# Attention and snake MLP on one core: moving one chunk's TensorE transposes from the first stage into the first product

## The chip, the cores and the metric

The kernel runs on one core of a Trainium2 chip. The metric is the time of one execution on the device, in microseconds (us), and lower is better. Four runs of the kernel before are shown: 437.31, 437.31, 438.04 and 438.66, with a median of 437.67.

The engines are named as the profile names them: PE is TensorE's matmul side and PEld its weight loads, DVE is VectorE, ACT is ScalarE, POOL is GpSimd, and SP issues most of the DMAs. Each engine works through its own instructions in the order in which the program has them.

## The reference

The inputs are q, k and v with 8 batches, 12 heads, 448 tokens and a head size of 64, two gain vectors g_q and g_k, and an MLP of 768 by 2048 and back.

```
q_n = q / sqrt(mean(q*q) + 1e-6) * g_q         # k_n likewise with g_k
attn = softmax(q_n @ k_n.T / 8) @ v            # per batch and head
x = attn as 3584 tokens x 768
h = x @ w_in                                   # 2048 wide
g = h + sin(alpha * h)**2 / alpha
out = g @ w_out
```

Matmuls take bf16 inputs and accumulate in f32.

## The kernel before

The 12 heads of a batch form 6 pairs of heads, and two pairs form a chunk, so a batch has 3 chunks (`NC` = 3) and the whole input has 24. Chunks are numbered through all batches: chunks 0 to 2 belong to the first batch, chunk 3 is the first one of the second batch, and in the code of the first stage c0 to c4 are the norms of chunks 0 to 4. In the change's title "fourth chunk" is chunk 3.

For each chunk the norm runs in steps: squares of q and k, sums of squares (`reduce`, L227, on DVE), the reciprocal root (`rsqrt`, L236 and L237, on ACT), folding both gains into q (L224, POOL), scaling (L246), and a transpose, so that the head dimension lies on the partitions (`qkT`). The first four chunks are transposed on PE (`pe_transpose`, L260 to L277): 28 transposes of 64x64 blocks into one PSUM bank pair `tp`, and two DVE copies from there to `qkT`. All later chunks go through a DMA transpose.

`scores` (L286) makes one of 7 key tiles of a chunk: four matmuls into a bank pair `sc`, and one exponential on ACT (L297) that writes `expT`. A batch has 21 of these score tiles. `attend` (L302) makes the values of one pair: per key tile four matmuls (the values and the row sums) that accumulate in a bank pair `av`, then `rec` (logarithm and exponential on ACT, L320 and L321) and two DVE multiplies that write `xT` (L326). In the program, `S_` is a score tile (a number in it adds that many warming matmuls on zeros), `A_()` is the values of one pair and `A_(2)` the values of the last two pairs interleaved.

`first_product` (L346), called h(b), makes h for a batch: 16 column tiles of 128, two to a bank pair `hps`, 6 matmuls each. The first two bank pairs are filled together, k-tile by k-tile, because the last `xT` come late. Each h tile goes through `snake`: a sine on ACT (L332), a square on POOL or ACT, and a DVE instruction that writes `g_sb` (L340) one h tile later. Tasks given in `beside` are emitted after the numbered pair of h tiles. `second_product` (L379) makes the output from `g_sb` and `w_out`; its matmuls (`ops`, L400) are the fillers of the next batch's stage, and each unit ends with a DVE copy `osb` (L406) and output DMAs.

PSUM is cut into four bank pairs. `bank_pair` (L97) hands out the one that is due first by times that the code itself adds up (`clock`, `passes`, `give_back`); an instruction that needs a bank still in use waits for it on the chip.

The first stage, batch 0's scores and values, is written out by hand (L484 to L532), and so is the order on PE, ACT and DVE there. From batch 1 on, the order within a stage is the string `PLAN` (L535), 83 items long; norm tasks of later chunks hang on 24 slots spread evenly over it. In the stage of batch b, n3 and n4 are the first two chunks of batch b + 1, whose norms are made beside it; their steps 3 and 4 are the two sums of squares (for q and for k).

Of the kernel before, what the change touches and what calls it, by code (L numbers as in the profile page):

```python
# [32 lines left out]
def kernel(  # L33
# [33 lines left out]
    NJ = S // REST  # L67
# [29 lines left out]
    def bank_pair(name, dtype=F32):  # L97
        slot = min(free_at, key=free_at.get)
        clock["pe"] = max(clock["pe"], free_at.pop(slot))
        ps = psum.tile([P, 2, 2048 // mybir.dt.size(dtype)], dtype, tag=f"ps{slot}", name=name)  # L100
        slot_of[id(ps)] = slot
        return ps

    def passes(pe=0.0, act=0.0):

        clock["pe"] += pe
        if act:
            clock["act"] = max(clock["act"], clock["pe"] + 0.25) + act
        return max(clock["pe"], clock["act"] if act else 0.0)

    def give_back(ps, time):
        free_at[slot_of.pop(id(ps))] = time
# [3 lines left out]
    def load_qk(ci, k_queue=nc.sync):  # L116

        b, dp = ci // NC, ci % NC
        qk[ci] = inp.tile([P, 2, 2 * NJ, D], F32, tag="qk", name="qk")
        for which, src, queue in ((0, q, nc.sync), (1, k, k_queue)):  # L120
            heads = src[b].rearrange("(hi dp pp) (p j) d -> dp (pp p) hi (j d)", hi=2, pp=2, j=NJ)[dp]
            queue.dma_start(out=qk[ci][:, which].rearrange("p (hi j) d -> p hi (j d)", hi=2), in_=heads)

    def key_rows(pi, hi):

        r = (hi + pi) % 2
        return slice(r * 64, r * 64 + 64)

    def load_v(b):

        vb[b] = vpool.tile([P, NP, NJ, D], BF16, tag="vb", name="vb")
        tok = v[b].rearrange("(hi dp pp) (p j) d -> hi pp p dp (j d)", hi=2, pp=2, j=NJ)
        slots = vb[b].rearrange("p (dp pp) j d -> pp p dp (j d)", pp=2)
        parts = [(slots[pp][key_rows(pp, hi)], tok[hi, pp]) for pp in range(2) for hi in range(2)]
        return [lambda o=o, i=i: nc.gpsimd.dma_start(out=o, in_=i) for o, i in parts]
# [150 lines left out]
    def scores(c, j, warm=0):  # L286

        sc = bank_pair("sc")
        for _ in range(warm):
            nc.tensor.matmul(sc[:, 0], blank[:, :P], blank, start=True, stop=True)  # L290
        for pp in range(2):
            for hi in range(2):
                qkt, r = qkT[2 * c + pp], slice(hi * 64, hi * 64 + 64)
                nc.tensor.matmul(sc[key_rows(pp, hi), pp, :S], qkt[r, 1, j * REST:(j + 1) * REST], qkt[r, 0, :],  # L294
                                 start=True, stop=True)
        expT[c, j] = epool.tile([P, 2, S], BF16, tag="expT", name="expT")
        nc.scalar.activation(expT[c, j], sc[:, :, :S], ACT.Exp, scale=SCALE)  # L297
        give_back(sc, passes(0.2 + 0.2 * warm, 0.82) + 0.2)
# [3 lines left out]
    def attend(pi, tiles=range(NJ)):  # L302


        b, hp = pi // NP, pi % NP
        if tiles[0] == 0:
            avs[pi] = bank_pair("av")
        av = avs[pi]
        for j in tiles:
            for part in range(2):  # L310
                for hi in range(2):
                    r = key_rows(pi, hi)
                    o = slice((hi + part) % 2 * 64, (hi + part) % 2 * 64 + 64)
                    nc.tensor.matmul(av[o, part, :S], ones[r, :] if part else vb[b][r, hp, j, :],  # L314
                                     expT[pi // 2, j][r, pi % 2, :], start=(j == 0), stop=(j == NJ - 1))
        passes(0.19 * len(tiles))
        if tiles[-1] < NJ - 1:
            return
        rec = rpool.tile([P, S], F32, tag="rec", name="rec")
        nc.scalar.activation(rec, av[:, 1, :S], ACT.Ln)  # L320
        nc.scalar.activation(rec, rec, ACT.Exp, scale=-1.0)  # L321
        if hp == 0:
            xT[b] = xpool.tile([P, KT, S], BF16, tag="xT", name="xT")
        for hi in range(2):
            r, o = slice(hi * 64, hi * 64 + 64), slice(64 - hi * 64, 128 - hi * 64)
            nc.vector.tensor_mul(xT[b][r, hp, :], av[r, 0, :S], rec[o, :])  # L326
        give_back(avs.pop(pi), passes(0.0, 1.06) + 1.4)
# [94 lines left out]
    def fill(n):  # L422
        for _ in range(min(n, len(fillers))):
            fillers.popleft()()
# [30 lines left out]
    def begin_norm(ci):  # L455
        norm[ci] = norm_tasks(ci)

    def step_of(ci, *steps):
        return lambda: [norm[ci].steps[n]() for n in steps]

    def beside_h(b):

        ci = NC * b + 5
        if ci >= NC * B:
            return {}
        return {0: [lambda: begin_norm(ci)], 1: [step_of(ci, 0)], 3: [step_of(ci, 1)], 4: [step_of(ci, 3)],
                MT // 2: [step_of(ci, 2, 4)]}

    def stage(b):

        tiles = deque((b * NC + c, j) for c in range(NC) for j in range(NJ))
        pairs = deque(b * NP + p for p in range(NP))

        def values(n=1):

            if n == 1:
                return attend(pairs.popleft())
            for j in range(NJ):
                for pi in list(pairs)[:n]:
                    attend(pi, [j])  # L480

        return (lambda warm=0: scores(*tiles.popleft(), warm)), values

    S_, A_ = stage(0)  # L484
# [15 lines left out]
    c3 = norm[NC]  # L500
# [6 lines left out]
    c4 = norm[NC + 1]  # L507
# [11 lines left out]
    S_(2)  # L519
    c3.scale(0), c3.scale(1)  # L520
    load_qk(NC + 3)
    S_(1), A_(), S_(1), S_(1)
    c3.pe_transpose((0, 1))
    A_(), S_()
    c4.reduce(0), c4.reduce(1)
    S_(), A_(2)
    c4.rsqrt()
    beside = beside_h(0)
    for i, task in ((2, lambda: c4.scale(0, [0])), (3, lambda: c4.scale(0, [1])), (4, lambda: c4.scale(1, [0])),
                    (5, lambda: c4.scale(1, [1])), (6, step_of(NC + 1, 6)), (6, beside[3].pop())):  # L530
        beside.setdefault(i, []).append(task)
    first_product(0, beside)  # L532
# [5 lines left out]
    for b in range(1, B):  # L538
        nc.scalar.preload_act_table_set(EXP_LN)
        clock["act"] = clock["pe"] + 3.3  # L540
        fillers.extendleft(reversed(second_product(b - 1)))

        n_fill = len(fillers) - (KEPT if b % 2 == 0 else 0)
        at = [[] for _ in range(SLOTS)]
        n2, n3, n4 = (NC * b + 2 + n for n in range(3))
        at[2].append(step_of(n2, 5))
        at[7].append(step_of(n2, 6))
        if b + 1 < B:
            at[2] += [lambda: begin_norm(n3), step_of(n3, 0, 1, 2)]
            at[10] += [lambda: begin_norm(n4), step_of(n4, 0, 1)]  # L550
            for slot, task in ((10, step_of(n3, 3)), (11, step_of(n3, 4)), (12, step_of(n3, 5)), (12, step_of(n4, 2)),
                               (14, step_of(n4, 3)), (15, step_of(n4, 4)), (17, step_of(n3, 6)), (18, step_of(n4, 5)),
                               (23, step_of(n4, 6))):
                at[slot].append(task)
            for n, part in enumerate(load_v(b + 1)):
                at[19 + n].append(part)
        S_, A_ = stage(b)
        due = slot = 0
        for n, x in enumerate(plan):
            while slot * len(plan) <= n * SLOTS:  # L560
                for task in at[slot]:
                    task()
                slot += 1
            if x == "F":
                due += n_fill
                fill(due // plan.count("F"))
                due %= plan.count("F")
            else:
                (S_ if x == "S" else A_)()
        for tasks in at[slot:]:  # L570
            for task in tasks:
                task()
        first_product(b, beside_h(b))
# [30 lines left out]
```

## Time and profile before

| | |
|---|---|
| median of the four runs | 437.67 us |
| the profiled execution | 437.31 us |
| its span, first to last instruction | 435.5 us |
| mean granted TensorE clock | 0.999 |
| PE busy | 423.5 us, 97% |
| ACT busy | 338.5 us, 78% |
| POOL busy | 279.6 us, 64% |
| DVE busy | 230.9 us, 53% |
| h(0) on PE | from 40.94 us, 96 matmuls |
| second stage's first `ops` on PE | from 59.11 us |

Times inside the execution count from the start of the span. In a group or in the order of time, a line gives start and length, engine, line of the code, operation, output and inputs, and in brackets how long the engine was idle before it and what ended that. The chain that ended last is followed back from the last instruction, at each step to what released it. Two entries of one engine that follow each other closely can overlap in their records, as an instruction starts before the one ahead of it has drained.

### The profile page before, as it was taken

Reading aid. Unit: us, or ns where it says so; the run is one execution under the profiler, and the core shown is the slowest. Engines: PE = TensorE matmul, PEld = TensorE weight load, DVE = VectorE, ACT = ScalarE, POOL = GpSimd, SP = SyncE. Lnnn points to the kernel's source line nnn. Section 1 sums busy time; section 2 is a strip of 40 time slices with the busy share of each in tenths; the row PEclk is TensorE's granted clock in tenths of the full one; section 3 lists DMA queues with packets and bytes.
Section 4 is the critical chain, followed back from the end, with each engine's and each line's share of the span. In section 5 each row is a group of like instructions: output and inputs, shape, how many; then the busy total and the mean of one; then the engine's idle time right before and its main releaser. Section 6 shows DMA issues by size and latency. Waiting matters only on the chain.

```text
span 435.5 us, 9511 instructions
## 1 busy us (share of the span) xinstructions
PE 423.5 (97%) x3845; PEld 220.8 (51%) x3845; DVE 230.9 (53%) x335; ACT 338.5 (78%) x529; POOL 279.6 (64%) x263
## 2 busy tenths in 40 slices
PE   7888999999999999999999999999999999999996
PEld 3345554555555555555555554555555555555563
DVE  4787563647454573556545564554636474246511
ACT  5887889778888787978889788887878788788600
POOL 4968789927896569928698269946599276002400
PEclk9999999999999999999999999999999999999999
DMA  7999998690249606692076903594064901320022
GB/s 254 214 253 221 210 202 205 151 258 18 56 149 218 153 0 112 135 231 97 2 200 182 191 1 75 150 229 121 1 187 93 126 0 29 89 56 2 0 66 80
DMA packets 68240, 54.63 MB, mean 125 GB/s; under 512 B 39636, under 2 KB 63972, under 8 KB 68196
## 3 DMA queue, kind: packets, MB, share of 16 engines
q1 hardware_dynamic: 54834, 40.51, 36.8%
q0 software_dynamic: 12416, 11.81, 17.6%
q10 hardware_dynamic: 946, 1.70, 1.0%
q8 instruction: 30, 0.49, 0.5%
q14 instruction: 14, 0.11, 0.1%
HBM read 45.62 MB, written 11.01 MB: 130 GB/s over the span
## 4 chain that ended last, share of the span: by engine, by line
PE 81%; ACT 2%; DVE 2%; issue 0%
PE ops L400 32%; PE hps L353 29%; PE av L314 13%; PE sc L294 7%; ACT expT L297 2%; DVE ms L227 1%; DVE osb L406 0%; DVE g_sb L340 0%; DVE xT L326 0%; ACT rec L321 0%; ACT inv L236 0%; ACT inv L237 0%; ACT rec L320 0%
## 5 line engine op out<-in xcount | busy, mean ns | idle before, releaser
L297 ACT ACTIVATE expT<-sc 128x896 bf16<-128x896 f32 x168 | 144.5, 913 | 28.9 <-PE sc L294 28.2
L400 PE MATMUL ops<-w_out_sb,g_sb 128*128 128x384 bf16 x896 | 156.6, 327 | 0.0
L353 PE MATMUL hps<-xT,w_in 128*128 128x448 bf16 x768 | 146.7, 353 | 0.0
L335 POOL TENSOR_TENSOR s<-s 128x448 f32<-128x448 f32 x64 | 59.5, 934 | 116.0 <-ACT s L332 102.5
L400 PEld LDWEIGHTS <-g_sb 128*128 128x128 bf16 x896 | 83.1, 98 | 70.0 <-issue 18.8
L340 DVE SCALAR_TENSOR_TENSOR g_sb<-s,inv_alpha_sb,hps 128x448 bf16<-128x448 f32 x128 | 80.8, 676 | 62.2 <-POOL s L335 62.2
L353 PEld LDWEIGHTS <-w_in 128*128 128x128 bf16 x768 | 74.5, 98 | 71.5 <-issue 2.9
L332 ACT ACTIVATE s<-hps,alpha_sb 128x448 f32<-128x448 f32 x128 | 74.6, 628 | 27.1 <-PE hps L353 25.3
L326 DVE TENSOR_TENSOR xT<-av,rec 64x448 bf16<-64x448 f32 x96 | 59.7, 622 | 66.3 <-ACT rec L321 47.2
L246 POOL TENSOR_TENSOR qkn<-qk,inv 128x448 bf16<-128x448 f32 x80 | 72.7, 940 | 7.4 <-POOL qk L224 7.0
L221 POOL TENSOR_TENSOR sq<-qk 128x896 f32<-128x896 f32 x44 | 73.4, 1686 | 0.0
L314 PE MATMUL av<-expT,vb 64*64 64x448 bf16 x672 | 69.2, 349 | 2.7 <-ACT expT L297 1.7
L314 PE MATMUL av<-expT,ones 64*64 64x448 bf16 x672 | 69.3, 349 | 0.0
L227 DVE TENSOR_REDUCE ms<-sq 128x14 f32<-128x896 f32 x44 | 46.8, 1081 | 16.4 <-POOL sq L221 16.1
L294 PE MATMUL sc<-qkT 64*64 64x448 bf16 x672 | 50.9, 361 | 1.7 <-DVE qkT L276 1.4
L406 DVE COPY osb<-ops 128x768 f32<-128x768 f32 (+1 forms) x33 | 27.6, 836 | 46.2 <-PE ops L400 39.7
L224 POOL TENSOR_TENSOR qk<-qk,gg 128x896 f32<-128x896 f32 x24 | 50.2, 2093 | 1.7 <-ACT gg L171 1.7
L314 PEld LDWEIGHTS <-vb 64*64 64x64 bf16 x672 | 37.8, 107 | 15.1 <-issue 3.5
L314 PEld LDWEIGHTS <-ones 64*64 64x64 bf16 x672 | 37.0, 107 | 11.1
L337 ACT ACTIVATE s<-s 128x448 f32<-128x448 f32 x64 | 36.9, 577 | 2.8
L320 ACT ACTIVATE rec<-av 128x448 f32<-128x448 f32 x48 | 26.1, 544 | 5.9 <-PE av L314 5.5
L294 PEld LDWEIGHTS <-qkT 64*64 64x64 bf16 x672 | 15.0, 105 | 29.6 <-issue 26.2
(44 smaller groups left out, 140.8 us busy)
## 6 DMA issues: line engine op xcount, KB each, us to landing
qk<-in_q_dram SPq DMA_DIRECT2D x24, 448.0 KB, 5.0
qk<-in_k_dram SPq DMA_DIRECT2D x22, 448.0 KB, 5.4
out_dram<-osb SPq DMA_DIRECT2D x39, 192.0 KB, 2.9
vb<-in_v_dram POOLq DMA_DIRECT2D x32, 168.0 KB, 6.4
w_in<-in_moe_w_in_dram POOLq DMA_DIRECT2D x4, 768.0 KB, 12.1
w_out_sb<-in_moe_w_out_dram POOLq DMA_DIRECT2D x2, 1536.0 KB, 23.4
out_dram<-osb SPq DMA_DIRECT2D x26, 96.0 KB, 4.5
qk<-in_k_dram ACTq DMA_DIRECT2D x2, 448.0 KB, 5.9
```

Of the source, the lines that this page charges most:

```text
L221: nc.gpsimd.tensor_mul(st.sq[w], qk[ci][:, w], qk[ci][:, w])
L227: nc.vector.reduce_sum(st.ms[:, w, :], st.sq[w], axis=AX.X)
L246: eng.tensor_mul(n[:, :, hi, :], x[:, hi], inv[:, hi].unsqueeze(2).to_broadcast([P, NJ, D]))
L294: nc.tensor.matmul(sc[key_rows(pp, hi), pp, :S], qkt[r, 1, j * REST:(j + 1) * REST], qkt[r, 0, :], start=True, stop=True)
L297: nc.scalar.activation(expT[c, j], sc[:, :, :S], ACT.Exp, scale=SCALE)
L314: nc.tensor.matmul(av[o, part, :S], ones[r, :] if part else vb[b][r, hp, j, :], expT[pi // 2, j][r, pi % 2, :], start=(j == 0), stop=(j == ...
L326: nc.vector.tensor_mul(xT[b][r, hp, :], av[r, 0, :S], rec[o, :])
L332: nc.scalar.activation(s1, hps, ACT.Sin, scale=alpha_sb[:, m, :])
L335: nc.gpsimd.tensor_mul(s2, s1, s1)
L340: nc.vector.scalar_tensor_tensor(g_sb[:, m, (b % 2) * S:(b % 2 + 1) * S], s2, inv_alpha_sb[:, m, :], hps, op0=ALU.mult, op1=ALU.add)
L353: nc.tensor.matmul(ps[:, m % 2, :S], w_in_sb[m * 2 // MT][:, kt, m % (MT // 2) * P:(m % (MT // 2) + 1) * P], x[:, kt, :], start=(kt == 0), ...
L400: nc.tensor.matmul(st["ps"][:, k, :HALF], g_sb[:, m, c0:c0 + P], w_out_sb[:, m, half * HALF:(half + 1) * HALF], start=(m == 0), stop=(m == ...
```

## The change

Three things are changed.

1. In the first stage the TensorE transposes of chunk 3 (`c3.pe_transpose`) leave their place ahead of the fourth pair's values, and are emitted in h(0) instead, after the first two bank pairs of h tiles (`beside`, index 0). The score tile that stood behind the fourth pair's values stands ahead of them now; the last score tile follows these values, and the two sums of squares of chunk 4 come behind it, ahead of the last two pairs' values.
2. `values(2)` makes the first six key tiles of one pair, then the first six of the other, and then the last key tile of both. Before, it went key tile by key tile through both pairs.
3. In the stages of batches 1 to 6, the first sum of squares of n4 hangs on slot 13 instead of 14. Slot 13 lies before the last of the eight fillers ahead of the first values of the stage; slot 14 lies behind these values.

```diff
-            for j in range(NJ):
+            for js in (range(NJ - 1), [NJ - 1]):
                 for pi in list(pairs)[:n]:
-                    attend(pi, [j])
+                    attend(pi, js)
...
-    S_(1), A_(), S_(1), S_(1)
-    c3.pe_transpose((0, 1))
-    A_(), S_()
+    S_(1), A_(), S_(1), S_(1), S_(), A_(), S_()
     c4.reduce(0), c4.reduce(1)
-    S_(), A_(2)
+    A_(2)
     c4.rsqrt()
     beside = beside_h(0)
-    for i, task in ((2, lambda: c4.scale(0, [0])), (3, lambda: c4.scale(0, [1])), (4, lambda: c4.scale(1, [0])),
+    for i, task in ((0, lambda: c3.pe_transpose((0, 1))), (2, lambda: c4.scale(0, [0])), (3, lambda: c4.scale(0, [1])), (4, lambda: c4.scale(1, [0])),
                     (5, lambda: c4.scale(1, [1])), (6, step_of(NC + 1, 6)), (6, beside[3].pop())):
...
-                               (14, step_of(n4, 3)), (15, step_of(n4, 4)), (17, step_of(n3, 6)), (18, step_of(n4, 5)),
+                               (13, step_of(n4, 3)), (15, step_of(n4, 4)), (17, step_of(n3, 6)), (18, step_of(n4, 5)),
```

## The prediction

> **What bounds the kernel now.** I read the page first: busy shares and the chain that ended last.
>
> ```profile
> PE 423.5 (97%) x3845; PEld 220.8 (51%) x3845; DVE 230.9 (53%) x335; ACT 338.5 (78%) x529; POOL 279.6 (64%) x263
> PE 81%; ACT 2%; DVE 2%; issue 0%
> ```
>
> TensorE (PE) is the bound, and from 80.08 us to the last output copy the chain names PE alone. So whatever PE gains or loses before 80 us arrives at the end one for one, and nothing after it can pay unless it creates a wait. Second view: what PE waited for from 30 us to 92 us. The same question from 92 us on has no row at all.
>
> ```profile
> PE av L314 <- ACT expT L297: 1.5, 1, 1.5
> PE av L314 <- DVE osb L406: 0.9, 1, 0.9
> PE sc L290 <- ACT expT L297: 0.4, 1, 0.4
> PE sc L294 <- ACT expT L297: 0.3, 1, 0.3
> ```
>
> The first two rows are the places that the change touches. Third view: the order of time, ACT, DVE and PE at the end of the first stage.
>
> ```profile
> 33.93 0.89 PE L269 MATMUL tp<-ident,qkn 64*128 64x64 bf16 x28
> ...
> 36.10 0.58 PE L294 MATMUL sc<-qkT 64*64 64x448 bf16 x8
> ...
> 38.36 0.38 PE L314 MATMUL av<-expT,vb 64*64 64x448 bf16 x2 [1.49 <-ACT expT L297]
> ...
> 33.83 1.71 ACT L297 ACTIVATE expT<-sc 128x896 bf16<-128x896 f32 x2
> 36.35 0.54 ACT L320 ACTIVATE rec<-av 128x448 f32<-128x448 f32 x1 [0.81 <-PE av L314]
> 36.92 0.58 ACT L321 ACTIVATE rec<-rec 128x448 f32<-128x448 f32 x1
> 37.41 1.71 ACT L297 ACTIVATE expT<-sc 128x896 bf16<-128x896 f32 x2
> 40.88 0.54 ACT L320 ACTIVATE rec<-av 128x448 f32<-128x448 f32 x1 [1.77 <-PE av L314]
> ...
> 38.82 2.08 DVE L227 TENSOR_REDUCE ms<-sq 128x14 f32<-128x896 f32 x2
> 42.07 2.55 DVE L326 TENSOR_TENSOR xT<-av,rec 64x448 bf16<-64x448 f32 x4 [1.17 <-ACT rec L321]
> ```
>
> ACT lies idle twice, and PE stands 1.49 us for the bank of score tile 20, whose exponential is queued behind the fourth pair's `rec`. h(0) starts at 40.94 and runs its 96 matmuls in 18.27 us without a gap. Fourth view: the chain before 80.08.
>
> ```profile
> 75.67 0.62 DVE xT L326
> 76.28 0.01 issue
> 76.30 0.63 DVE xT L326
> 76.93 0.03 issue
> 76.96 2.08 DVE ms L227 x2
> 79.04 0.03 issue
> 79.07 0.97 DVE osb L406
> 80.04 0.04 issue
> 80.08 1.52 PE av L314 x28
> ```
>
> Two sums of squares stand ahead of the output copy whose bank the next values need, while DVE had been idle for 3.32 us before the xT at 75.67.
>
> **Earlier scores and split values (first stage).** Tile 20's scores follow tile 19's at 33.9. By the code's bank bookkeeping they take the bank that the transposes had (freed when the scaling ended at 33.40); the fourth pair's values take tile 18's bank (exponential done at 34.69). So these values run as before, from 34.75 to 36.30. ACT does tile 20's exponential in its idle 0.81: 35.54 to 36.40 (two took 1.71). `rec` follows, to 37.46, then tile 21's exponential, to 38.36 (before: 39.12). The last two pairs' values start at 36.29 in tile 19's bank; six key tiles of one pair, then of the other, are 12 x 0.19 (28 matmuls take 1.32) = 2.28, to 38.57; the last key tile of both (needing 38.36) adds 0.38. h(0) starts at about 39.04 instead of 40.94: 1.90 earlier. Unshown is whether nothing else holds it: bounds 0 (a new wait takes it all) and 1.90. I take 1.90, since each exponential above comes before the values that read it.
>
> **What is late next.** DVE keeps the order xT of pair 4 (fourth), two sums, xT of pairs 5 and 6: 37.58 to 38.84, to 40.95 (2.08), to 42.25 and 43.53 (four took 2.55). `rec` of the last pair, shifted with PE, ends at 41.1, earlier. h(0) takes its k-tiles in order for its first two bank pairs, 16 matmuls x 0.19 = 3.05, so it wants xT 5 at 42.08 and gets it at 42.30 (0.21 lost), wants xT 6 at 43.06 and gets it at 43.58 (0.52 lost). The first 24 matmuls end at 44.34 instead of 45.51: of 1.90 remain 1.17. Bounds of this loss: 0 (sums not in the way) and 1.90 (xT as late as before); 0.73 is read from the DVE rows.
>
> **Transposes into h(0).** Out of the first stage go 28 PE instructions (0.85 from first to next) and two DVE copies (1.16 at 35.25): gain nothing, as PE would stand there for tile 18's bank until 34.69. In h(0) PE has no gap, so they cost at least 0.85 and, with a switch on either side, 0.07 each, 0.99: taken. Upper bound 1.25 with the 0.2 idle of the weight load seen at 33.93 on both sides. No DMA moves, and nothing on the SP or POOL queue. Their bank is that of pair 5's values (free at 42.25). The third h tile takes pair 6's bank, but the fourth takes the transposes' bank and waits for the two copies. On DVE these stand behind the first `g_sb`, before at 47.00, now 45.83, ending 46.47, so the copies end at 47.62. PE reaches the fourth tile at 44.34 + 0.99 + 2.28 = 47.61: 0.07 lost with the hand-over. Bounds: 0 and 2.29 (a whole tile, if it is met one tile earlier). Behind the copies the second `g_sb` ends at 48.25, and PE wants its bank at 49.96. End of h(0): 1.17 - 0.99 - 0.07 = 0.11 earlier.
>
> [...] The granted clock is 1.00 in the stretch that holds the transposes today and in h(0):
>
> ```profile
> 34.00:41.00 7.00, 5.51 (x121) 3.81 (x122) 5.68 (x8) 4.39 (x7) 6.98 (x8) 1.00 1.07 217
> 45.50:59.20 13.70, 13.70 (x74) 7.12 (x73) 8.96 (x14) 11.72 (x21) 12.05 (x13) 1.00 1.30 204
> ```
>
> [...]
>
> **One sum of squares from slot 14 to 13.** In the second stage it goes ahead of the xT, into the 3.32 us of idle DVE. Its square ends at 73.23 + 1.66 = 74.89 on POOL; the sum runs 74.92 to 75.99 and xT waits 0.32 behind it (end 77.25; its readers come in h(1), and no bank of it is wanted before 78). The second sum follows to 78.30. The copy's last matmul ends at 78.35, so the copy runs 78.38 to 79.34 and PE goes on at 79.39 instead of 80.08: 0.69 gained. PE was ready at 79.01 (the eight score matmuls at 72.31 let the next go 0.40 later), so bounds are 0 and 1.07. In the five later stages that have this sum PE waits for nothing, and DVE is idle for 3.47 us before this xT, with the square done 2 us ahead of it: nothing. Without that cover it would be 5 x 1.04.
>
> **Sum.** 0.11 + 0.69 = 0.80 us. The profiled execution took 437.31 (span 435.5 and 1.8 around it), so its like would take 436.51 with a span of 434.7; the median of the runs shown stands 0.36 above it, at 437.67, which gives 436.87. About 0.3% (1.31 us) is what a measurement of this kernel can tell from no change.
>
> **The rivals.**
> - *Larger gain.* The xT come in time and the copies hide: 1.90 - 0.85 + 1.07 = 2.12, so 435.55. For it: ACT's idle 1.77 does go. Against: the two sums stand ahead of xT 5 and 6 in DVE's order.
> - *Nothing.* The copy at 79.07 is held by its own matmuls or by the later xT, and xT waits take h(0)'s gain: 0 to 0.1, so 437.6. For it: only 0.08 lies between the end of the second sum and the start of the copy. Against: the chain runs through the sums, not through `ops`.
> - *Slower.* h(0)'s third tile, not its fourth, gets the transposes' bank. PE would reach it at 45.33 and the copies end at 47.62: 2.29 lost, -0.80 + 2.29 = +1.49, so 439.16. It turns into a loss once PE waits over 0.80 us for that bank. For it: the copies wait for the sine, the POOL square and a `g_sb` before them. Against: by the code's times pair 6's bank falls due 3.3 us before the transposes' one.
>
> **How the numbers follow.** Likeliest 0.55, larger gain 0.20, nothing 0.12, slower 0.13. The likeliest alone reaches from 436.4 (the xT waits halved) to 437.5 (0.69 halved, transposes at 1.25). The range runs from 435.5, which takes in the larger gain, to 438.1, which takes in nothing-changed with the spread of the runs shown (437.31 to 438.66); it leaves out the slower case and a tail below. Faster by over 0.3% (below 436.36): the larger gain and an edge of the likeliest, 0.22. Slower by over 0.3%: 0.13. Within: 0.65.
>
> **What would show it.** Right: no PE wait of 1.5 us at 38; first h matmul at about 39.0 with two gaps of 0.2 and 0.5 before 43.6, released by DVE xT; 28 transposes near 44.4 in 0.9; at most 0.2 idle before the fourth h tile, released by DVE qkT; h(0) ending at about 59.1; one sum ahead of xT near 75, and the values at 79.4. Wrong: a PE wait for DVE qkT near 45 or over 0.8 us; a clock under 0.95 between 44 and 50; a new PE wait after 92 us; or h(0) starting later than 40.

## The result and the profile after

The changed kernel takes 436.64 us (median of 34 runs, 436.46 to 438.92) against 437.44 us (median of 55 runs of the kernel before, 437.13 to 439.64). The ratio is 0.9983 with a 95% interval of 0.9977 to 0.9989: 0.80 us by the medians, a gain that is clear of noise and smaller than 0.3%. The profiled execution took 436.48 us with a span of 434.7 us.

First the same question as before, what PE waited for from 30 us to 92 us of the changed kernel; from 92 us on there is again no row.

```profile
PE av L314 <- ACT expT L297: 0.6, 1, 0.6
PE hps L353 <- DVE xT L326: 0.4, 1, 0.4
PE sc L290 <- ACT expT L297: 0.4, 1, 0.4
PE sc L294 <- ACT expT L297: 0.3, 1, 0.3
PE av L314 <- DVE osb L406: 0.3, 1, 0.3
```

The wait of 1.5 us is gone, a smaller one has appeared earlier on ACT, a new one on `xT` stands in h(0), and the wait for the output copy fell from 0.9 to 0.3. The order of time of PE, ACT and DVE around the end of the first stage of the changed kernel:

```profile
33.55 0.57 PE L294 MATMUL sc<-qkT 64*64 64x448 bf16 x8
34.72 0.38 PE L314 MATMUL av<-expT,vb 64*64 64x448 bf16 x2 [0.60 <-ACT expT L297]
...
39.01 4.09 PE L353 MATMUL hps<-xT,w_in 128*128 128x448 bf16 x20
43.47 0.92 PE L353 MATMUL hps<-xT,w_in 128*128 128x448 bf16 x4 [0.37 <-DVE xT L326]
44.32 0.89 PE L269 MATMUL tp<-ident,qkn 64*128 64x64 bf16 x28
45.14 13.91 PE L353 MATMUL hps<-xT,w_in 128*128 128x448 bf16 x72
58.89 1.30 PE L400 MATMUL ops<-w_out_sb,g_sb 128*128 128x384 bf16 x7
...
33.77 2.52 ACT L297 ACTIVATE expT<-sc 128x896 bf16<-128x896 f32 x3
36.28 0.55 ACT L320 ACTIVATE rec<-av 128x448 f32<-128x448 f32 x1
...
38.76 2.08 DVE L227 TENSOR_REDUCE ms<-sq 128x14 f32<-128x896 f32 x2
40.87 2.55 DVE L326 TENSOR_TENSOR xT<-av,rec 64x448 bf16<-64x448 f32 x4
```

ACT now runs three exponentials in a row and goes on without a pause to `rec`. h(0) starts at 39.01 instead of 40.94, but where the kernel before needed 18.17 us from its first h matmul to the first `ops`, this one needs 19.88: a wait for `xT`, which DVE makes only after the two sums, and the transposes. So h(0) ends at 58.89 instead of 59.11. The chain ahead of the values in the second stage, of the changed kernel:

```profile
74.72 0.04 DVE ms L227
74.76 1.08 issue
75.84 0.62 DVE xT L326
76.46 0.01 issue
76.47 0.63 DVE xT L326
77.10 0.03 issue
77.13 1.09 DVE ms L227
78.22 0.03 issue
78.25 0.97 DVE osb L406
79.22 0.04 issue
79.26 1.52 PE av L314 x28
```

One sum (the 0.04 and the 1.08 called "issue") stands ahead of `xT` and one behind it. The values start at 79.26 instead of 80.08; from there on PE waits for nothing in either kernel, and the spans differ by the same 0.8 us.

### The profile page after: what moved, and what is told of

It reads as the page before. It is cut to its first block, busy times and chain, and to the rows that moved or that the text cites. A ratio compares the mean times of both kernels' runs of the same rounds, so it can differ in the third digit from the quotient of the medians.

```text
span 434.7 us, 9516 instructions
## 1 busy us (share of the span) xinstructions
PE 424.5 (98%) x3845; PEld 220.9 (51%) x3845; DVE 231.4 (53%) x335; ACT 338.6 (78%) x529; POOL 279.8 (64%) x263
## 4 chain that ended last, share of the span: by engine, by line
PE 81%; POOL 2%; DMA 1%; DVE 1%; issue 1%
PE ops L400 32%; PE hps L353 29%; PE av L314 13%; PE sc L294 7%; DMA qkT<-qkn 1%; POOL sq L221 1%; POOL qkn L246 1%; POOL qk L224 0%; DVE osb L406 0%; DVE xT L326 0%; DVE ms L227 0%
## 5 line engine op out<-in xcount | busy, mean ns | idle before, releaser
L224 POOL TENSOR_TENSOR qk<-qk,gg 128x896 f32<-128x896 f32 x24 | 50.2, 2093 | 1.5 <-ACT gg L171 1.5
```

The costliest lines, as they stand in the source:

```text
L224: eng.tensor_mul(qk[ci][:, 0], qk[ci][:, 0], gg.to_broadcast([P, 2 * NJ, D]))
```

## The experiments

Each kernel was timed beside the kernel before on the same chip: the first seven on one chip, the next two on a second and the last two on a third. So times are compared with the kernel before in the same line, and kernels of different chips by their ratios. "Low clock" below means a run whose mean granted TensorE clock was 0.996 or less. Such runs occur in all kernels: of 75 runs of the kernel before beside these experiments, fifteen had one. Where an h tile is said to get a bank or to start, it is a bank pair of h(0) with its two column tiles, 12 matmuls.

**The slot alone.** On the kernel before:

```diff
- ... (14, step_of(n4, 3)), (15, step_of(n4, 4)), ...
+ ... (13, step_of(n4, 3)), (15, step_of(n4, 4)), ...
```

> The kernel before with the sum of squares on slot 13 alone. My theory: the second stage's output copy starts at 78.4 instead of 79.07 and PE's wait of 0.89 us for it shrinks to 0.2 to 0.3; 0.6 to 0.7 us faster (ratio 0.9985), h(0) unchanged. Rival (the copy is held by its own matmuls, and the gain of the whole change is the first stage's): no change, the values at 80.1 as before.

Measured: 436.81 us against 437.39, ratio 0.9984 (0.9971 to 0.9997), a span of 434.9 us. The DVE order of this kernel:

```profile
74.90 1.08 DVE L227 TENSOR_REDUCE ms<-sq 128x14 f32<-128x896 f32 x1 [2.60 <-POOL sq L221]
76.02 1.26 DVE L326 TENSOR_TENSOR xT<-av,rec 64x448 bf16<-64x448 f32 x2
77.31 1.08 DVE L227 TENSOR_REDUCE ms<-sq 128x14 f32<-128x896 f32 x1
78.42 0.96 DVE L406 COPY osb<-ops 128x768 f32<-128x768 f32 x1
```

The copy starts at 78.42 instead of 79.07. This one number in the list of slots carries 0.58 us of the 0.80.

**The first stage and h(0) alone.** The changed kernel, with the slot back at 14:

```diff
- ... (13, step_of(n4, 3)), (15, step_of(n4, 4)), ...
+ ... (14, step_of(n4, 3)), (15, step_of(n4, 4)), ...
```

> The changed kernel with the sum of squares back on slot 14. My theory: h(0) starts at 39.0 and ends 0.1 to 0.2 us earlier than before, the wait of 0.89 us for the copy stands; 0.1 to 0.2 us faster than before (ratio 0.9996). Rival (the first stage carries the gain): 0.7 us faster, the copy comes earlier without the slot.

Measured: 437.42 us against 437.39, ratio 0.9993 (0.9977 to 1.0009). The time alone can't tell it from no change. Its trace agrees with the small gain: it starts 0.27 us later than the trace of before at score tile 19 (33.88 against 33.61) and 0.11 us later after h(0) (59.22 against 59.11), so it gains 0.16 us in between. PE's wait of 0.9 us for the copy is there in full.

**The split values alone.** On the kernel before, transposes and score tiles where they were:

```diff
-            for j in range(NJ):
+            for js in (range(NJ - 1), [NJ - 1]):
                 for pi in list(pairs)[:n]:
-                    attend(pi, [j])
+                    attend(pi, js)
```

> The kernel before with the values of the last two pairs split as in the change, and nothing else: the transposes stay in the first stage. My theory: PE fills 1.14 us of the 1.49 us wait with the first pair's values, h(0) starts near 39.95, no xT comes late, and with no transposes inside h(0) ends 1.0 us earlier; ratio 0.9977, more than the whole first-stage part of the change. Rival (moving the transposes is what lets the rest gain): under 0.3 us, since the last score tiles come as late as before.

Measured: 436.54 us against 437.39, ratio 0.9974 (0.9963 to 0.9986). This one part gains about as much as the whole change. PE in this kernel's order of time:

```profile
37.27 0.37 PE L314 MATMUL av<-expT,ones 64*64 64x448 bf16 x2
37.30 0.35 PE L314 MATMUL av<-expT,vb 64*64 64x448 bf16 x2
38.38 0.38 PE L314 MATMUL av<-expT,vb 64*64 64x448 bf16 x2 [0.73 <-ACT expT L297]
```

The wait shrank by 0.76, from 1.49 to 0.73, and not by the 1.14 that I had expected. From 36.51 on PE does five key tiles of the first pair and then stops: the sixth needs score tile 20, whose exponential ends only then. One of the five had already run ahead of the wait before, so 4 x 0.19 = 0.76 are filled. h(0) then runs from 40.21 to 58.38 without a gap (18.17), since the sums on DVE are over before the `xT` are due.

**Split values and the slot.** The two edits just shown, together:

```diff
+            for js in (range(NJ - 1), [NJ - 1]):
...
+ ... (13, step_of(n4, 3)), (15, step_of(n4, 4)), ...
```

> The kernel before with the split values and slot 13, transposes left in the first stage. My theory: the two terms add, 1.0 + 0.65 = 1.65 us faster than before (ratio 0.9962), so 0.85 us faster than the changed kernel. Rival: 0.7 to 0.9 us, no better than the changed kernel.

Measured: 436.05 us against 437.39, ratio 0.9966 (0.9952 to 0.9979), a span of 434.1 us: 1.34 us faster. In the trace the two terms add: h(0) ends 0.76 earlier than in the kernel before, counted from score tile 19 in both (58.29 - 33.55 against 59.11 - 33.61), and the wait for the copy is 0.3 instead of 0.9. By the medians the two edits alone give 0.85 and 0.58, together 1.43. With the transposes left in the first stage the kernel is 0.6 us shorter in its span than the changed one; the intervals of the two ratios (0.9952 to 0.9979 and 0.9977 to 0.9989) just touch.

**The sums early.** The changed kernel, with chunk 4's sums ahead of the fourth pair's values:

```diff
-    S_(1), A_(), S_(1), S_(1), S_(), A_(), S_()
-    c4.reduce(0), c4.reduce(1)
-    A_(2)
+    S_(1), A_(), S_(1), S_(1), S_()
+    c4.reduce(0), c4.reduce(1)
+    A_(), S_(), A_(2)
```

> The changed kernel with chunk 4's two sums of squares ahead of the fourth pair's values, where DVE is idle for over 2 us. My theory: the xT of the last two pairs no longer wait behind the sums, the wait of 0.37 us inside h(0) goes, and the kernel is 0.4 us faster than the changed one, 1.2 us faster than before (ratio 0.9973). Rival (the xT are late because of ACT, not because of the sums): the wait stays, ratio 0.9983.

Measured: 435.89 us against 437.31, ratio 0.9966 (0.9954 to 0.9978). The profiled execution had a low clock between 21.7 and 25.2 us, so its times stand 0.9 us late (score tile 19 starts at 34.47, in the changed kernel at 33.55); stretches after that can be compared. The row by stretches (the third number from the right is the granted clock), then DVE and PE:

```profile
22.00:24.00 2.00, 2.00 (x28) 1.15 (x20) 0.99 (x3) 0.89 (x3) 2.00 (x2) 0.50 1.07 251
...
36.10 2.08 DVE L227 TENSOR_REDUCE ms<-sq 128x14 f32<-128x896 f32 x2
38.39 1.26 DVE L326 TENSOR_TENSOR xT<-av,rec 64x448 bf16<-64x448 f32 x2 [0.21 <-ACT rec L321]
41.05 2.54 DVE L326 TENSOR_TENSOR xT<-av,rec 64x448 bf16<-64x448 f32 x4 [1.40 <-ACT rec L321]
...
39.93 4.71 PE L353 MATMUL hps<-xT,w_in 128*128 128x448 bf16 x24
44.57 0.89 PE L269 MATMUL tp<-ident,qkn 64*128 64x64 bf16 x28
```

The four `xT` wait for ACT now, not for the sums, and the wait in h(0) is gone. From the first h matmul to the transposes it is 4.64 us, against 5.31 in the changed kernel: 0.67 us, though the trace had called the wait there 0.37. A matmul's record is 0.35 long while the next starts 0.19 later, so a gap between records is 0.16 shorter than the time lost, and a shorter loss does not show at all. In the changed kernel the first 20 h matmuls have a group of 4.09, where 19 x 0.19 + 0.35 would be 3.96: 0.13 lost at the fifth `xT`. With 0.37 + 0.16 = 0.53 at the sixth that makes the 0.67.

**Everything ahead, transposes in the first stage.** On the kernel before, with the split values and the slot:

```diff
     c3.pe_transpose((0, 1))
-    A_(), S_()
+    S_()
     c4.reduce(0), c4.reduce(1)
-    S_(), A_(2)
+    A_(), S_(), A_(2)
```

> The kernel before with the split values, slot 13, the next-to-last score tile and the two sums ahead of the fourth pair's values, and the transposes left in the first stage ahead of that score tile. My theory: the fourth pair's values start 0.5 us later, at 35.25, h(0) starts near 39.5, nothing is late in it and it holds no transposes; 1.4 + 0.65 = 2.0 us faster than before (ratio 0.9954). Rival (the transposes cost in the first stage what they cost in h(0)): 1.2 us faster, as the changed kernel with early sums.

Measured: 435.40 us against 437.31, ratio 0.9958 (0.9944 to 0.9972), a span of 433.4 us. It beats both kernels: its interval lies wholly below that of the change. PE in this kernel:

```profile
39.43 18.33 PE L353 MATMUL hps<-xT,w_in 128*128 128x448 bf16 x96
57.60 1.79 PE L400 MATMUL ops<-w_out_sb,g_sb 128*128 128x384 bf16 x10
```

The kernel with early sums differs from this one only in where the transposes stand. There h(0) took 19.21 us to the first `ops`, here 18.17: 1.04 us for the transposes. Counted from score tile 19 (34.47 there, 33.48 here), h(0) starts 0.49 us earlier there than here. So the transposes' move buys 0.49 us at the start of h(0) and costs 1.04 inside; the medians (435.89 and 435.40, same chip) say the same.

**The bank met one tile earlier.** The changed kernel, with the transposes' bank due 4.3 us sooner in the code's times, so that the third h tile gets it. This builds the slower rival of the prediction:

```diff
-        def pe_transpose(pairs, ws=(0, 1), act=False):
+        def pe_transpose(pairs, ws=(0, 1), act=False, due=1.3):
...
-            give_back(tp, passes(1.0) + 1.3)
+            give_back(tp, passes(1.0) + due)
...
-(0, lambda: c3.pe_transpose((0, 1)))
+(0, lambda: c3.pe_transpose((0, 1), due=-3.0))
```

> The changed kernel, with the transposes' bank marked as due 4.3 us sooner in the code's own times, so that h(0)'s third tile gets it instead of the fourth. My theory: PE waits 2.3 us near 45.1 for the two DVE copies, and the kernel ends 2.2 to 2.4 us later than the changed one, 1.4 to 1.6 us later than before (ratio 1.0034). Rival (the copies would come as soon as PE needs them): as the changed kernel, ratio 0.9983.

Measured: 440.40 us against 437.31, ratio 1.0071 (1.0055 to 1.0086), twice the expected loss. The wait is as expected, in the one run of six with a clock of 1.0:

```profile
44.44 0.89 PE L269 MATMUL tp<-ident,qkn 64*128 64x64 bf16 x28
47.65 13.79 PE L353 MATMUL hps<-xT,w_in 128*128 128x448 bf16 x72 [2.32 <-DVE qkT L276]
```

That run took 438.84 us, 1.53 more than the median before. By start times the wait costs 2.39: 47.65 - 44.44, less the 0.82 that lie between the same two starts in the changed kernel. The other five had mean clocks of 0.991 to 0.996 and took 439.94 to 441.48.

**The same kernel, for a trace with a low clock.** Nothing is edited.

> The kernel with the transposes' bank due early, unchanged, once more, for a profile of an execution with a lowered clock: of its six runs five had a mean granted clock of 0.991 to 0.996 and took 1.1 to 2.6 us more than the sixth. My theory: the clock falls to half for some 3 to 4 us right after the wait of 2.3 us, near 48. Rival: it falls elsewhere, near 24 as in one profile of the early sums, and has nothing to do with the wait.

Measured: one run, 440.04 us, with a mean clock of 0.996. The table by stretches; the third number from the right is the granted clock:

```profile
44.00:46.00 2.00, 1.19 (x30) 0.77 (x28) 0.30 (x1) 1.94 (x4) 0.93 (x1) 1.00 1.32 208
46.00:48.00 2.00, 0.49 (x2) 0.27 (x3) 2.00 (x5) 1.42 (x3) 1.61 (x2) 0.70 1.31 204
48.00:50.00 2.00, 2.00 (x7) 0.77 (x6) 1.22 (x3) 0.00 (x0) 0.96 (x1) 0.50 1.32 205
50.00:52.00 2.00, 2.00 (x11) 1.03 (x10) 0.00 (x0) 0.69 (x2) 0.00 (x0) 0.94 1.29 203
```

The clock falls to half during the wait (in stretches of 0.25 us it is 1.00 up to 46.75, 0.63 up to 47.00 and 0.50 from there on) and comes back at 50.2: (0.30 x 2 + 0.50 x 2 + 0.06 x 2) / 0.5 = 3.4 us at half speed. The 72 h matmuls behind it take 15.12 instead of 13.79: 1.33, about the 1.20 by which this run is longer than the undisturbed 438.84. So in this run the rest of the loss is the clock, and it fell during the wait. The other low-clock runs have no trace. One stretch of 3.4 us at half speed takes 0.004 off the mean of a 438 us run, which is the 0.996 seen here; a mean of 0.991 needs two, and where the second lies is not shown. The clock's fall can have another cause, too: in the trace with the early sums it fell at 21.7, as long and as deep, and the longest PE wait in the 3.4 us ahead of it is 0.72 us.

**The wait filled with matmuls on zeros.** The same kernel, and between the transposes and the third h tile:

```diff
-            give_back(tp, passes(1.0) + due)
+            time = passes(1.0) + due
+            if due < 0:
+                fill_ps = bank_pair("ps")
+                for _ in range(11):
+                    nc.tensor.matmul(fill_ps[:, 0, :blank.shape[-1]], blank[:, :P], blank, start=True, stop=True)
+                give_back(fill_ps, clock["pe"] + 1.0)
+            give_back(tp, time)
```

> The same kernel with eleven warming matmuls on zeros (11 x 0.22 = 2.4 us) in the other free bank, between the transposes and the wait. My theory (PE's idleness lowers the clock): the third h tile starts at the same time, 47.6, the low clocks get as rare as in the kernel before, and the median falls to the one undisturbed run's 438.8, ratio 1.0034. Rival (the low clock is chance, or comes from the late h tiles): ratio 1.007 as without the filling.

Measured: 439.27 us against 437.41, ratio 1.0045 (1.0031 to 1.006). The third h tile starts at 47.58 as without the filling, but only one of six runs had a low clock, and the lowest times are 438.80 and 438.84. Two more runs took 440.3 at clocks of 0.998 and 0.999, which this does not explain; the kernel before has such runs too (438.59 at a clock of 1.0 among the eleven beside it).

**Plain matmuls in the transposes' place.** Here four plain matmuls lead up to the wait. Is a low clock then as frequent as with transposes, or about as rare as in the kernel before? Two theories, one for each answer, were set against each other. The transposes come three pairs of h tiles later:

```diff
+    scratch = const.tile([P, 2, S], BF16, name="scratch")
...
+    def plain():
+        ps = bank_pair("fk")
+        for n in range(4):
+            nc.tensor.matmul(ps[:, n % 2], blank[:, :P], blank, start=True, stop=True)
+        for n in range(2):
+            nc.vector.tensor_copy(scratch[:, n], ps[:, n, :S])
+        give_back(ps, passes(1.0) - 3.0)
...
-(0, lambda: c3.pe_transpose((0, 1)))
+(0, plain), (4, lambda: c3.pe_transpose((0, 1)))
```

> The changed kernel with four plain matmuls on zeros (4 x 0.22 us) and two DVE copies of 448 columns from their bank to a scratch tile in the transposes' place in h(0), that bank due early as in the two kernels before; the transposes follow three pairs of h tiles later, at their normal due time. PE waits some 2.2 us for the copies as there, but plain matmuls instead of transposes lead up to the wait. Theory A (the wait alone lowers the clock): low clocks in most runs, as with the transposes (six of seven). [...] Time of an undisturbed run about 438.9 by both.

Measured: 439.71 us against 437.22, ratio 1.0061 (1.0043 to 1.0078), with a wait of 2.28 us. The expected 438.9 had forgotten that this kernel holds both the plain matmuls and the transposes, 0.8 us more work. One of six runs had a low clock, and it is the profiled one: there the clock stood at 0.82, 0.50 and 0.82 in the three stretches of 2 us from 46 to 52 us, again 3.4 us at half speed; it fell at 47.3, just before the wait ended at 47.42. One more run took 441.34 at a clock of 1.0, which is not explained.

**Beside it, the kernel with the early bank again.** Nothing is edited here either.

> The kernel with the transposes' bank due early, again, beside the kernel with plain matmuls on the same chip, to compare how often the clock is low. Both theories: low clocks in most runs, median 440.0 to 440.4, ratio 1.006 to 1.007.

Measured: 440.22 us, ratio 1.0062 (1.0042 to 1.0083); four of six runs had a low clock. Together with the two experiments before, that makes ten of thirteen with transposes ahead of the wait, against fifteen of 75 in the kernel before: a low clock is more frequent with the two together. With plain matmuls ahead of the wait it is one of six. On this one chip, where the two can be compared directly, it is four of six against one of six, which chance can give. That the transposes have a part in it is a hint, no more; the single low clock after plain matmuls may be of the kind that the kernel before has.

## Why the prediction was right

The range held the time (436.64; 436.87 was named), the likeliest case came, and its mechanism is what the runs show. By its steps:

- *h(0) starts 1.90 earlier.* 39.01 was measured for 39.04, and ACT ran the three exponentials and `rec` in the order and without the pause that were forecast. The changed kernel's trace already stands 0.06 ahead at score tile 19, so the gain is 1.87.
- *0.73 lost to late xT.* 0.67, by the run with early sums. Its cause, the two sums ahead of `xT` on DVE, is shown by moving them: the four `xT` then wait for ACT, and the loss is gone (ratio 0.9966 against 0.9983). The prediction expected two gaps of 0.2 and 0.5 in the records; by start times 0.13 and 0.53 are lost, and the record shows 0.37, because the overlap hides the rest.
- *0.99 for the transposes, 0.07 for their bank.* From the 24th h matmul to the 25th: the last of the first 24 starts at 43.47 + 3 x 0.19 = 44.04, so the next could at 44.23 and does at 45.14: 0.91, which leaves 0.06 for the two switches that were put at 0.07 each. The remaining 72 take 13.75 to the first `ops`, where 72/96 of 18.17 would be 13.63: 0.12. Together 1.03 for 1.06. (The prediction's 18.27 for h(0)'s matmuls is the length in later batches; to the first `ops` it is 18.17. No sum uses it.)
- *0.11 earlier at the end of h(0).* 0.22 in the trace, less the 0.06: 0.16; timed alone, it can't be told from no change.
- *0.69 from the slot.* 0.60 in the trace (80.08 to 79.26, less 0.22), 0.58 alone. `xT` came 0.39 after its old place, where 0.32 was expected, so the second sum ended late, at 78.22, and the chain has the copy right behind it at 78.25. It was expected at 78.38, less 0.22: the 0.09 are missing here. The prediction's 78.35 for the end of the copy's matmuls is the start of the last of them. The rival that the slot brings nothing fell with the slot alone.
- *No change to later stages.* There is no row of PE waiting after 92 us.
- *The clock.* The 28 transposes of 64x64 take 0.89 us in h(0), as they did in the first stage (0.89 from 33.93), and the clock from 44 to 50 us is 1.00. The prediction's row of 28 in 0.89 was the right one for the price.
- *The slower rival.* Its price, 2.29 for the bank, was right where the clock held (2.32 in the records, 2.39 by start times). Its total was too small for most runs, because with such a wait behind the transposes the clock is low more often (ten of thirteen runs, against fifteen of 75). The prediction had no row for a wait of that length.
- *The larger gain.* It did not come, for the reason given against it: the sums stand ahead of `xT` 5 and 6.

That 0.80 was named and 0.80 measured is in part luck: the first-stage part came out 0.05 above its term and the slot 0.09 below, and 0.06 of the 0.8 between the two spans is the lead that the changed kernel's trace had before the change begins. The time named lies 0.23 too high because the four runs shown had a higher median than the 55 (437.67 and 437.44). And its 1.31 us for what a measurement can tell from no change was too coarse: the interval here is 0.06%, 0.26 us, to either side.

What the prediction did not see is that the parts pull against each other. Its sum has 1.90 gained and 1.79 lost inside the first-stage part, and it took both as given. The runs show that the loss was a choice. The change's first-stage part gains 0.16 in the trace, the split alone 0.76 (0.85 by the medians). With the slot, the change gives 0.80; with the transposes left in the first stage and the sums early it is 1.91.

## What to carry to other kernels

Ask of work on the engine that is the bound whether that engine has a gap there. In h(0), where PE had none, the 28 transposes cost 1.04 us, their full length (0.89 in the record) and a little more. Taken from the first stage, where PE would wait anyway, they gave back less (0.49). Look first for idle places on the engine that is waited for. Here DVE, whose sums and `xT` stand in the traces in the program's order, was idle ahead of `xT` in two places (2.32 us at 37.47 in the changed kernel, 3.32 us at 75.67 in the kernel before), and using these was worth more than moving TensorE work (0.67 us inside h(0), 0.58 in the second stage): a sum that is due soon goes ahead of the instruction that waits, not behind it. And take the loss at a wait from start times, not from the gap between records.

## What the runs showed of the hardware

With a wait of 2.3 us on PE in the middle of dense matmuls and 0.9 us of transposes before it, ten of thirteen runs had a low clock, against fifteen of 75 of the kernel before. Six of the seven runs on the first two chips and four of six on the third were low; on the first and the third they took 1.1 to 2.6 us more than the best run there. The wait is not enough by itself: in two traces with it (2.32 us) the clock stayed at 1.00. Nor is it needed: in the trace with early sums the clock fell with no PE wait over 0.72 us in the 3.4 us ahead of it. Each of the three traces with a low clock holds one stretch at 0.50, of 3.4 us. With matmuls on zeros in place of the wait, the third h tile started at the same time (47.58), and the low clock came in one run of six. With four plain matmuls ahead of a wait of 2.28 us it was one of six, too. Ten of thirteen against one of six is a hint that the transposes have a part in it, no more.
